# A pointwise convolution kernel: x's first chunk goes ahead of pw on SyncE's queue, one weight eviction is split between two engines, and weight copies are made once

## The chip, the cores and the metric

The kernel runs on one core of a Trainium2 chip. The metric is the device time of one execution in microseconds. The engines are TensorE (PE, with its weight loads shown as PEld), VectorE (DVE), ScalarE (ACT), GpSimd (POOL) and SyncE (SP), which here only issues DMAs.

## The reference

x is 1 x 384 x 384 x 384 in bf16 (147,456 pixels of 384 channels), dw is 1 x 1 x 384 and pw is 384 x 384. With k = 1 the depthwise step is one factor for each channel:

```
out = x * dw[0, 0]                             # one factor for each channel
return jnp.einsum('bhwc,cd->bhwd', out, pw)    # 384 x 384 matrix for each pixel
```

## The kernel before

The pixels are cut into 288 supertiles of 512. x is loaded in chunks of 1, 1, 1, 1, 2, 4, 5, 5 supertiles, then of 10, and of fewer at the end (`chunks`, from `_groups`), into three buffers `Xs`. VectorE transposes each supertile as 32-bit words in 32 x 32 blocks from X into `Ts` (lines 367 and 369), in two halves of three blocks; only the very first half is three instructions of one block each, with semaphores `s_t` and `s_tb`, so that PE may begin after the first block. PE does 48 matmuls for a supertile (line 225): 12 steps, each with four matmuls in four row groups of 32, which write the four banks of one half of PSUM (`PS[0]` or `PS[1]`, in turn). ScalarE evicts the four banks in one instruction into `Os` (line 429), and SyncE stores them.

The matmuls need the weights `w_r`: pw scaled by dw and spread over the row groups. They are made at the start. dw is loaded on ScalarE's queue, turned to a column by three small matmuls (line 255) and copied to `dw_f`. VectorE makes `sel_w`, a selection matrix scaled by dw, for each third k of the channels (line 400). PE multiplies it with pw (`pw_n`, which shares a tile named `raw` with `sel_w`) for k = 0, 1, 2 and r = 0, 1 (line 275): six pieces i = 2k + r, each of two banks, v = 0 and 1. The pieces go to PSUM and are evicted by `w_out` (line 385) into `w_r`; `w_eng` says which engine takes each piece (1 is ScalarE, 0 is VectorE; semaphores `s_wr`). Pieces 4 and 5 use the banks of pieces 0 and 1 and wait for their eviction. `times` makes PE do the two pieces of k = 2 twice over. The first supertile needs pieces 0 to 3 at its first step, piece 4 at its ninth step and piece 5 at its eleventh (`w_first`).

Before that, `idle_work` gives PE matmuls on constants (line 242): four rounds at the very start, two after the matmuls on dw. PE then waits for pw's first 128 rows (`s_pw`) and, ahead of k = 1, for the rest (`s_pw2`).

SyncE issues in this order: pw's first 128 rows (line 179), the rest of pw (line 180), x's chunk 0 (line 181, issued at line 133), x's chunks 1 to 5, then, after chunk 1 has landed, the rest of the loads and stores by a sorted list. Semaphores of a DMA count 16 at its landing.

On VectorE the order at the start is: `sel` (line 390), `dw_f` (397), `sel_w` (400), the weight pieces that are VectorE's, then the transposes of supertile 0 and of supertile 1. On ScalarE it is its weight pieces, then the evictions of the supertiles.

Of the kernel before, what the change touches and what calls it, by code (L numbers as in the profile page):

```python
# [26 lines left out]
def kernel(  # L27
# [12 lines left out]
    nc = tc.nc  # L40
# [38 lines left out]
    w_r = consts.tile([P, NB, 2, D], BF16, name="w_r")  # L79
# [31 lines left out]
    s_wr = [nc.alloc_semaphore(f"s_wr{e}") for e in range(2)]  # L111

    with tc.tile_critical(sync_engine=mybir.EngineType.Pool, no_gpsimd_drain=True):  # L113
        def x_of(t):
            g, i, off, first, L = chunks[t]
            if first + 2 == NS:
                return Xl[:], s_xl, 32
            n = sum(len(ls) > i for ls in groups[g % NR : g + 1 : NR])
            return Xs[g % NR][:, 4 * off : 4 * (off + L), :], s_x[g % NR][i], 16 * n

        def load_x(t, eng=nc.sync):
            g, i, off, first, L = chunks[t]
            dst, sem, _ = x_of(t)
            rows = xf[512 * first : 512 * (first + L), :]
            if first + 3 < NS:
                src = rows.rearrange("(p s) c -> p (s c)", p=P)
                dst = dst.rearrange("p s c -> p (s c)")
                if i == 0 and g >= NR:
                    je = g_end[g - NR]
                    eng.wait_ge(s_t[je % 2][1], je // 2 + 1)  # L130
            else:
                src = rows.rearrange("(a k q) c -> q a k c", k=4, q=4)
            eng.dma_start(dst, src).then_inc(sem, 16)  # L133
# [38 lines left out]
            eng = nc.scalar if first + 1 == NS and k == 2 else nc.sync  # L172
            eng.dma_start(dst, src).then_inc(s_o[g % NR], 16)

        w_eng = [1, 0, 1, 1, 1, 1]
        w_all = [(s_wr[e], w_eng.count(e)) for e in range(2)]

        nc.scalar.dma_start(dw_row[:], dw.rearrange("a e c -> a (e c)")).then_inc(s_dw, 16)
        nc.sync.dma_start(pw_n[:, 0], pw[0:P, :]).then_inc(s_pw, 16)  # L179
        nc.sync.dma_start(pw_n[:, 1:3], pw[P:C, :].rearrange("(k p) d -> p k d", p=P)).then_inc(s_pw2, 16)  # L180
        load_x(0)

        todo = []
        for t, (g, i, off, first, L) in enumerate(chunks):
# [12 lines left out]
        for o in sorted(range(NR), key=lambda o: (len(groups) - 1 - o) % NR):  # L197
            n = sum(n_parts[t] for t, c in enumerate(chunks) if c[0] % NR == o)
# [3 lines left out]

        w_done = [(s_wr[e], w_eng[: i + 1].count(e)) for i, e in enumerate(w_eng)]

        w_first = {(0, 0): [(0, 1), (1, 3)], (4, 0): [(1, 4)], (4, 1): [(1, 5)]}

        def w_ps(i):
            return PS[0 if i in (2, 3) else 1][:, 2 * (i % 2) : 2 * (i % 2) + 2, :D]  # L210
# [4 lines left out]
        def supertile(s, rv):  # L215
            for b, par in steps:
                for q in range(4):
                    if q == 0 and par == 0 and b in (0, 3):
                        nc.tensor.wait_ge(s_t[s][b // 3], rv)
                    if q == 0 and s == 0:  # L220
                        for e, v in w_first.get((b, par), []):
                            nc.tensor.wait_ge(s_wr[e], v)
                        if par == 0 and b in (1, 2):
                            nc.tensor.wait_ge(s_tb, b)
                    mm = nc.tensor.matmul(  # L225
                        PS[s][:, q, :D],
                        lhsT=Ts[s][32 * q : 32 * q + 32, b, par::2],
                        rhs=w_r[32 * q : 32 * q + 32, b, par, :],
                        start=(b, par) == steps[0],
                        stop=(b, par) == steps[-1],  # L230
                        tile_position=(32 * q, 0),
                    )
                    if (b, par) == steps[0] and q == 0:
                        mm._wait_ge(s_a[s], rv)
                    if (b, par) in ((2, 1), (5, 1)) and q == 3:
                        mm.then_inc(s_pe)


        def idle_work(n):
            for _ in range(n):  # L240
                for i in range(4):
                    nc.tensor.matmul(  # L242
                        PS[0][:, 2 * (i % 2) + i // 2, :D],
                        lhsT=ones[32 * i : 32 * i + 32, 0:P],
                        rhs=ones[32 * i : 32 * i + 32, :],
                        start=True,
                        stop=True,
                        tile_position=(32 * i, 0),
                    )
# [10 lines left out]
                stop=True,  # L260
            )
        mm.then_inc(s_df)
        idle_work(2)
        nc.tensor.wait_ge(s_pw, 16)
        times = {(2, 0): 2, (2, 1): 2}
        for k in range(3):
            if k == 1:
                nc.tensor.wait_ge(s_pw2, 16)
            nc.tensor.wait_ge(s_sw, k + 1)
            for r in range(2):  # L270
                if k == 2:
                    nc.tensor.wait_ge(*w_done[r])

                for v in [0, 1] * times.get((k, r), 1):
                    mm = nc.tensor.matmul(  # L275
                        PS[(k + 1) % 2][:, 2 * r + v, :D],
                        lhsT=sel_w[64 * v : 64 * v + 64, k, r, :, :].rearrange("p q w -> p (q w)"),
                        rhs=pw_n[64 * v : 64 * v + 64, k, :],
                        start=True,
                        stop=True,  # L280
                        tile_position=(64 * v, 0),
                    )
                mm.then_inc(s_w)
        with nc.tensor.Fori(0, NS // 2 - 1, 1) as it:
            rv = nc.tensor.to_reg(it + 1)
            for s in range(2):
                supertile(s, rv)
        supertile(0, NS // 2)

        Tk = Ts[1][:].rearrange("p b (i r) -> p (b i) r", r=2)  # L290
# [15 lines left out]
        for m in range(4):  # L306
# [14 lines left out]
            out=eye[:],  # L321
            in_=ones[:, 0:P],
# [20 lines left out]
        def transposes(t, j):  # L343
            g, i, off, first, L = chunks[t]
            jj = first + j
            s = jj % 2
            if jj + 1 == NS:
                nc.vector.wait_ge(s_xk, 32)
                Tw = Ts[s][:].bitcast(U32).rearrange("p b (m w) -> p (b m) w", w=32)
                for v in range(2):  # L350
                    blocks = slice(12 * v, 12 * v + 12)
                    ins = nc.vector.transpose(out=Tw[:, blocks], in_=Xk[:, blocks].bitcast(U32))  # L352
                    ins._wait_ge(s_pe, 2 * (jj - 2) + v + 1)
                    ins.then_inc(s_t[s][v])
                return
            X, sem, n = x_of(t)
            Xw = X.bitcast(U32).rearrange("p (k l) c -> p k l c", l=L)
            Tw = Ts[s][:].bitcast(U32).rearrange(
                "p b (k i) -> p b k i" if t < 2 else "p b (i k) -> p b k i", k=4
            )  # L360
            for h in range(2):
                if h == 0 and j == 0:
                    nc.vector.wait_ge(sem, n)
                if h == 0 and jj == 0:
                    for b in range(3):
                        x_b = Xw[:, :, 0, 32 * b : 32 * b + 32]
                        nc.vector.transpose(out=Tw[:, b], in_=x_b).then_inc(s_tb if b else s_t[0][0])  # L367
                    continue
                ins = nc.vector.transpose(  # L369
                    out=Tw[:, 3 * h : 3 * h + 3],  # L370
                    in_=Xw[:, :, j, 96 * h : 96 * h + 96].rearrange("p k (b w) -> p b k w", w=32),
                )
                if jj >= 2:
                    ins._wait_ge(s_pe, 2 * (jj - 2) + h + 1)
                ins.then_inc(s_t[s][h])
# [3 lines left out]

        order = [(t, j) for t in range(NT) for j in range(chunks[t][4])]  # L380

        def w_out(i):
            e, k, r = w_eng[i], i // 2, i % 2
            out, in_ = w_r[:, 2 * k : 2 * k + 2, r, :], w_ps(i)
            o = nc.vector.tensor_copy(out, in_) if e == 0 else nc.scalar.copy(out, in_)  # L385
            o._wait_ge(s_w, i + 1)
            o.then_inc(s_wr[e])
# [3 lines left out]
            out=sel[:],  # L391
            in_=eye[:].rearrange("p (v w r) -> p r w v", v=2, r=2),
# [6 lines left out]
        for k in range(3):  # L399
            nc.vector.tensor_scalar_mul(  # L400
                sel_w[:, k], sel[:].unsqueeze(2).to_broadcast([P, 2, 4, 32]), dw_f[:, k : k + 1]
            ).then_inc(s_sw)
        for i in range(6):
            w_out(i)
        transposes(*order[0])
        transposes(*order[1])

        for jj, (t, j) in enumerate(order):
            g, i, off, first, L = chunks[t]
# [28 lines left out]
            if jj + 2 < NS:  # L438
                transposes(*order[jj + 2])
# [30 lines left out]
```

## Time and profile before

| | |
|---|---|
| time before, median of 3 runs | 573.7 us (573.59 to 574.26) |
| profiled execution, span from the first to the last instruction | 572.6 us |
| profiled execution's own time | not given beside its span; the median of the runs is 1.1 us above the span |
| PE busy | 567.1 us, 99% of the span |
| DVE busy | 508.6 us, 89% |
| ACT busy | 418.3 us, 73% |
| DMA | 226.88 MB, mean 396 GB/s |
| first supertile's matmuls start | 6.45 us |
| second supertile's matmuls start | 9.02 us |

In the profile's rows times are microseconds unless marked ns. A row of the timeline has the start, the duration, the engine, the line of the kernel, the operation, the tiles written and read, the number of instructions merged into the row, and in brackets the engine's idle time before them with what ended it. A row of the chain of waits has start and duration. A row of the stretches has the stretch, its length, the busy time of PE, PEld, DVE, ACT and POOL with the number of instructions, the granted TensorE clock, the share of the DMA engines and the GB/s. A row of the DMA issues ends with the kilobytes of one and the median time from issue to landing. "SPq" is SyncE's queue of instructions. PE's matmuls are pipelined and their ends are modelled, so rows of PE overlap.

### The profile page before, as it was taken

What the parts mean: (1) busy time and instruction counts of PE and PEld (TensorE: products, weight loads), DVE (VectorE), ACT (ScalarE), POOL (GpSimd) and SP (SyncE); (2) the same over time, 40 slices, a digit from 0 to 9 for tenths busy, and PEclk for the clock granted to TensorE, in tenths of its full rate; (3) what the DMA queues carried; (4) which work ended last, traced back from release to release, by engine and by line L of the source; (5) the groups of instructions that cost most, each with busy time, mean ns of one, the idle gap of its engine ahead of it and who ended that gap; (6) DMA issues with size and microseconds to landing.
All of it is one profiled execution on the core that took longest, in us unless ns stands there. A gap on an engine that the chain in (4) does not pass through costs nothing.

```text
span 572.6 us, 29713 instructions
## 1 busy us (share of the span) xinstructions
PE 567.1 (99%) x13843; PEld 417.0 (73%) x13843; DVE 508.6 (89%) x588; ACT 418.3 (73%) x298; POOL 13.9 (2%) x41
## 2 busy tenths in 40 slices
PE   8999999999999999999999999999999999999997
PEld 4777777777777777777777777777777777777775
DVE  6999999999899899899899899899899899899895
ACT  6777777777777777777777777777777777777775
POOL 2042000000000000000000000000000000000000
PEclk9999999999999999999999999999999999999999
DMA  8999999999999999999999999999999999998777
GB/s 320 439 387 391 439 418 429 434 430 414 429 433 411 396 392 430 390 387 398 432 374 395 419 410 413 400 416 412 393 407 433 388 398 386 424 402 325 308 286 262
DMA packets 28084, 226.88 MB, mean 396 GB/s; under 512 B 1449, under 2 KB 7850, under 8 KB 24106
## 3 DMA queue, kind: packets, MB, share of 16 engines
q1 hardware_dynamic: 27140, 225.91, 97.5%
q10 hardware_dynamic: 934, 0.89, 0.4%
q14 instruction: 9, 0.07, 0.0%
q8 instruction: 1, 0.02, 0.0%
HBM read 113.54 MB, written 113.25 MB: 396 GB/s over the span
## 4 chain that ended last, share of the span: by engine, by line
PE 98%; DMA 1%; SPq 0%; issue 0%; DVE 0%; ACT 0%; POOLq 0%
PE ps L225 97%; DMA X<-in_x_dram 1%; PE ps L310 0%; PE ps L298 0%; DVE T L369 0%; ACT O L424 0%; SPq L133 0%; SPq L180 0%; SPq L179 0%; SPq L465 0%; POOLq L113 0%; POOLq L454 0%
## 5 line engine op out<-in xcount | busy, mean ns | idle before, releaser
L225 PE MATMUL ps<-w_r,T 32*128 32x384 bf16 x13776 | 560.0, 321 | 0.7 <-DVE T L369 0.4
L369 DVE STREAM_TRANSPOSE T<-X 128x384 uint32<-128x384 uint32 x571 | 500.6, 878 | 54.7 <-DMA X<-in_x_dram 1.1
L225 PEld LDWEIGHTS ps<-w_r,T 32*128 32x128 bf16 x13776 | 414.3, 93 | 146.6 <-issue 1.6
L429 ACT CAST O<-ps 128x1536 bf16<-128x1536 f32 x286 | 411.3, 1438 | 147.6 <-PE ps L225 147.6
L339 POOL COPY Xk<-Xl 32x256 bf16<-32x256 bf16 x16 | 6.3, 394 | 0.0
L338 POOL COPY Xk<-Xl 32x128 bf16<-32x128 bf16 x16 | 4.6, 287 | 25.5 <-DMA Xl<-in_x_dram 24.6
L385 ACT CAST w_r<-ps 128x768 bf16<-128x768 f32 x5 | 3.6, 820 | 0.8 <-PE ps L275 0.8
L333 POOL COPY raw<-w_r 32x768 bf16<-32x768 bf16 x4 | 3.3, 819 | 6.4 <-ACT w_r L385 6.2
L242 PE MATMUL ps<-const-bfloat16-1.0 32*128 32x384 bf16 x24 | 2.2, 515 | 1.1 <-PEq L454 1.1
L275 PE MATMUL ps<-raw 64*128 64x384 bf16 x16 | 2.8, 500 | 0.1
L275 PEld LDWEIGHTS ps<-raw 64*128 64x128 bf16 x16 | 0.8, 113 | 2.3 <-DMA raw<-in_pw_dram 1.2
L341 ACT ACT_TABLE_LOAD x1 | 1.3, 1283 | 1.5 <-PEq L454 1.5
L420 DVE CAST O<-ps 128x384 bf16<-128x384 f32 x2 | 1.0, 552 | 1.4 <-PE ps L225 1.4
L369 DVE STREAM_TRANSPOSE T<-Xl 128x384 uint32<-128x384 uint32 x2 | 1.8, 882 | 0.2
L242 PEld LDWEIGHTS ps<-const-bfloat16-1.0 32*128 32x128 bf16 x24 | 0.7, 117 | 1.4 <-issue 1.4
L390 DVE TENSOR_REDUCE sel<-eye 128x64 f32<-128x128 bf16 x1 | 0.3, 289 | 1.5 <-POOL eye L320 1.5
L352 DVE STREAM_TRANSPOSE T<-Xk 128x384 uint32<-128x384 uint32 x2 | 1.2, 578 | 0.5 <-PE ps L225 0.4
L310 PE MATMUL ps<-raw,T 128*128 128x384 bf16 x8 | 1.5, 328 | 0.0
L424 ACT CAST O<-ps 128x384 bf16<-128x384 f32 x2 | 1.0, 478 | 0.7 <-PE ps L310 0.7
L367 DVE STREAM_TRANSPOSE T<-X 128x128 uint32<-128x128 uint32 x3 | 0.7, 283 | 0.8 <-DMA X<-in_x_dram 0.8
L385 DVE CAST w_r<-ps 128x768 bf16<-128x768 f32 x1 | 1.0, 958 | 0.5 <-PE ps L275 0.5
L424 DVE CAST O<-ps 128x384 bf16<-128x384 f32 x2 | 1.1, 557 | 0.1
(14 smaller groups left out, 5.4 us busy)
## 6 DMA issues: line engine op xcount, KB each, us to landing
X<-in_x_dram SPq DMA_DIRECT2D x25, 3840.0 KB, 22.6
out_dram<-O SPq DMA_DIRECT2D x25, 3840.0 KB, 28.1
X<-in_x_dram SPq DMA_DIRECT2D x3, 1536.0 KB, 19.2
X<-in_x_dram SPq DMA_DIRECT2D x2, 1920.0 KB, 14.5
out_dram<-O SPq DMA_DIRECT2D x2, 1920.0 KB, 24.4
out_dram<-O SPq DMA_DIRECT2D x2, 1536.0 KB, 13.6
X<-in_x_dram SPq DMA_DIRECT2D x6, 384.0 KB, 6.4
out_dram<-O SPq DMA_DIRECT2D x3, 768.0 KB, 6.6
```

The costliest lines, as they stand in the source:

```text
L225: mm = nc.tensor.matmul(PS[s][:, q, :D], lhsT=Ts[s][32 * q : 32 * q + 32, b, par::2], rhs=w_r[32 * q : 32 * q + 32, b, par, :], start=(b, ...
L242: nc.tensor.matmul(PS[0][:, 2 * (i % 2) + i // 2, :D], lhsT=ones[32 * i : 32 * i + 32, 0:P], rhs=ones[32 * i : 32 * i + 32, :], start=True ...
L275: mm = nc.tensor.matmul(PS[(k + 1) % 2][:, 2 * r + v, :D], lhsT=sel_w[64 * v : 64 * v + 64, k, r, :, :].rearrange("p q w -> p (q w)"), rhs ...
L310: mm = nc.tensor.matmul(PS[1][:, m, :D], lhsT=Tk[:, P * (m + 2) : P * (m + 3), par], rhs=w_k[:, par, :], start=False, stop=par == 1,)
L333: nc.gpsimd.tensor_copy(w_k[quads[n]], w_r[quads[n], n]).then_inc(s_wk)
L338: nc.gpsimd.tensor_copy(Xk[quads[n], g:8:4, :], x_b).then_inc(s_xk)
L339: nc.gpsimd.tensor_copy(Xk[quads[n], 8 + g : 24 : 4, :], Xl[quads[g], :, 64 * n : 64 * n + 64]).then_inc(s_xk)
L341: nc.scalar.copy(warm[:, s : s + 1], nc.const_aps.tensor(0.0, [P, 1], F32)).then_inc(s_a[s])
L369: ins = nc.vector.transpose(out=Tw[:, 3 * h : 3 * h + 3], in_=Xw[:, :, j, 96 * h : 96 * h + 96].rearrange("p k (b w) -> p b k w", w=32),)
L385: o = nc.vector.tensor_copy(out, in_) if e == 0 else nc.scalar.copy(out, in_)
L424: o = (nc.scalar.copy if n % 2 else nc.vector.tensor_copy)(Ov[:, n, j, :], PS[s][:, n, :D])
L429: a = nc.scalar.copy(Ov[:, :, j, :], PS[s][:, :, :D])
```

## The change

x's chunk 0 is issued on SyncE's queue ahead of the two loads of pw instead of behind them. The fourth weight piece (i = 3) is evicted in two parts: its first bank by ScalarE, in ScalarE's order as before, its second by VectorE, between the first and the second block transpose of supertile 0; the waits of the first supertile count the two parts. The two pieces of k = 2 are multiplied once instead of twice, and the second `idle_work` has four rounds instead of two.

```diff
-        w_eng = [1, 0, 1, 1, 1, 1]
-        w_all = [(s_wr[e], w_eng.count(e)) for e in range(2)]
+        w_units = [(0, 0, 2, 1), (1, 0, 2, 0), (2, 0, 2, 1), (3, 0, 1, 1), (3, 1, 2, 0), (4, 0, 2, 1), (5, 0, 2, 1)]
+
+        def w_after(i):
+            n = [sum(u[3] == e and u[0] <= i for u in w_units) for e in range(2)]
+            return [(s_wr[e], n[e]) for e in range(2)]
+
+        w_all = w_after(5)
 
         nc.scalar.dma_start(dw_row[:], dw.rearrange("a e c -> a (e c)")).then_inc(s_dw, 16)
+        load_x(0)
         nc.sync.dma_start(pw_n[:, 0], pw[0:P, :]).then_inc(s_pw, 16)
         nc.sync.dma_start(pw_n[:, 1:3], pw[P:C, :].rearrange("(k p) d -> p k d", p=P)).then_inc(s_pw2, 16)
-        load_x(0)
...
-        w_done = [(s_wr[e], w_eng[: i + 1].count(e)) for i, e in enumerate(w_eng)]
-
-        w_first = {(0, 0): [(0, 1), (1, 3)], (4, 0): [(1, 4)], (4, 1): [(1, 5)]}
+        w_first = {(0, 0): w_after(3), (4, 0): w_after(4)[1:], (4, 1): w_after(5)[1:]}
...
-                        for e, v in w_first.get((b, par), []):
-                            nc.tensor.wait_ge(s_wr[e], v)
+                        for sem, v in w_first.get((b, par), []):
+                            nc.tensor.wait_ge(sem, v)
...
-        idle_work(2)
+        idle_work(4)
         nc.tensor.wait_ge(s_pw, 16)
-        times = {(2, 0): 2, (2, 1): 2}
         for k in range(3):
...
                 if k == 2:
-                    nc.tensor.wait_ge(*w_done[r])
-
-                for v in [0, 1] * times.get((k, r), 1):
+                    nc.tensor.wait_ge(*w_after(r)[1 - r])
+
+                for v in range(2):
...
                         nc.vector.transpose(out=Tw[:, b], in_=x_b).then_inc(s_tb if b else s_t[0][0])
+                        if b == 0:
+                            w_out(3, 1, 2, 0)
...
-        def w_out(i):
-            e, k, r = w_eng[i], i // 2, i % 2
-            out, in_ = w_r[:, 2 * k : 2 * k + 2, r, :], w_ps(i)
+        def w_out(i, v0, v1, e):
+            k, r = i // 2, i % 2
+            out, in_ = w_r[:, 2 * k + v0 : 2 * k + v1, r, :], w_ps(i)[:, v0:v1]
...
-        for i in range(6):
-            w_out(i)
+        for u in w_units:
+            if u[:2] != (3, 1):
+                w_out(*u)
```

## Prediction

> **What bounds the kernel now.** I read the page first, for the engine that fills the span. PE is busy 99% of it, and one group holds nearly all of that:
>
> ```profile
> PE 567.1 (99%) x13843; PEld 417.0 (73%) x13843; DVE 508.6 (89%) x588; ACT 418.3 (73%) x298; POOL 13.9 (2%) x41
> L225 PE MATMUL ps<-w_r,T 32*128 32x384 bf16 x13776 | 560.0, 321 | 0.7 <-DVE T L369 0.4
> ```
>
> Then the chain of waits that ended last, to see where PE stops being fed by itself:
>
> ```profile
> 1.87 0.46 SPq L133
> ...
> 2.38 5.89 DMA X<-in_x_dram
> ...
> 8.29 0.59 DVE T L369
> ...
> 9.02 557.88 PE ps L225 x13728
> 566.90 0.65 PE ps L298 x16
> ```
>
> From 9.02 us to 566.90 us PE never waits. Four matmuls with different row groups run together, so 13728 matmuls are 3432 groups of four, at 557.88 / 3432 = 0.1626 us each; a supertile of 512 rows is 12 groups, 1.95 us. The change touches nothing inside that stretch (the waits of the loop stay as many), nor the tail after it. So the whole question is one number: when the second supertile starts, now 9.02 us, and every tenth that this moves appears at the end of the kernel.
>
> The chain says that the second supertile waits for x's second chunk, issued at 2.38 and landed 5.89 us later, at 8.27. The timeline of the first 9 us shows what lies beside that (start, duration, engine, line; the bracket is the idle time before and its releaser):
>
> ```profile
> 0.96 0.39 SPq L179 DMA_DIRECT2D raw<-in_pw_dram  x1
> ...
> 1.12 1.47 PE L242 MATMUL ps<-const-bfloat16-1.0 32*128 32x384 bf16 x16 [1.12 <-PEq L454]
> ...
> 1.41 0.41 SPq L180 DMA_DIRECT2D raw<-in_pw_dram  x1
> ...
> 2.50 0.80 PE L242 MATMUL ps<-const-bfloat16-1.0 32*128 32x384 bf16 x5
> ...
> 3.37 2.83 PE L275 MATMUL ps<-raw 64*128 64x384 bf16 x16
> ...
> 3.91 3.61 ACT L385 CAST w_r<-ps 128x768 bf16<-128x768 f32 x5 [0.80 <-PE ps L275]
> 3.97 0.17 PEld L275 LDWEIGHTS ps<-raw 64*128 64x128 bf16 x4 [0.47 <-DMA raw<-in_pw_dram]
> 4.23 0.96 DVE L385 CAST w_r<-ps 128x768 bf16<-128x768 f32 x1 [0.48 <-PE ps L275]
> ...
> 6.04 0.70 DVE L367 STREAM_TRANSPOSE T<-X 128x128 uint32<-128x128 uint32 x3 [0.85 <-DMA X<-in_x_dram]
> ...
> 6.45 2.13 PE L225 MATMUL ps<-w_r,T 32*128 32x384 bf16 x48 [0.25 <-DVE T L367]
> 6.66 0.54 DVE L369 STREAM_TRANSPOSE T<-X 128x384 uint32<-128x384 uint32 x1
> ```
>
> The first supertile starts at 6.45, released by x's first chunk, and could hand over to the second at 6.45 + 1.95 = 8.40. It has 9.02 - 8.40 = 0.62 us of slack before x's second chunk stops being the bound: it may start as late as 7.07 at no cost.
>
> A second thing is in these rows: PE's pace.
>
> ```profile
> L242 PE MATMUL ps<-const-bfloat16-1.0 32*128 32x384 bf16 x24 | 2.2, 515 | 1.1 <-PEq L454 1.1
> 5.13 1.07 PE L275 MATMUL ps<-raw 64*128 64x384 bf16 x6
> ```
>
> The 16 matmuls of line 242 are 4 groups in 1.47 us, and with the 0.5 us of one matmul's own length (mean 515 ns) taken off, three steps take about 0.96, so 0.32 us a group, half the later speed. Line 225 at 6.45 does 11 steps in 2.13 - 0.32 = 1.81 us, 0.165 each. So between 1.12 and about 6 us PE runs at half speed, and from 6.45 at full speed. The column of the granted clock reads 1.00 throughout and does not show this; I go by the pace.
>
> **Part 1: x's first chunk ahead of pw.** What the queue gives, by size and by time to landing (each row is the one issue at 0.96, 1.41, 1.87, 2.38), and what the DMA engines moved per half microsecond:
>
> ```profile
> raw<-in_pw_dram SPq DMA_DIRECT2D x1, 96.0 KB, 2.0
> raw<-in_pw_dram SPq DMA_DIRECT2D x1, 192.0 KB, 2.5
> X<-in_x_dram SPq DMA_DIRECT2D x1, 384.0 KB, 4.1
> X<-in_x_dram SPq DMA_DIRECT2D x1, 384.0 KB, 5.9
> 2.00:2.50 0.50, 0.50 (x14) 0.21 (x10) 0.00 (x0) 0.50 (x1) 0.00 (x0) 1.00 0.66 174
> 2.50:3.00 0.50, 0.50 (x15) 0.10 (x7) 0.29 (x2) 0.49 (x3) 0.00 (x0) 1.00 0.81 186
> 3.00:3.50 0.50, 0.43 (x6) 0.16 (x4) 0.50 (x3) 0.11 (x2) 0.00 (x0) 1.00 1.37 313
> 3.50:4.00 0.50, 0.50 (x6) 0.03 (x4) 0.25 (x1) 0.09 (x1) 0.00 (x0) 1.00 0.71 169
> 4.00:4.50 0.50, 0.50 (x6) 0.14 (x4) 0.27 (x1) 0.50 (x1) 0.00 (x0) 1.00 0.85 344
> 4.50:5.00 0.50, 0.48 (x5) 0.16 (x4) 0.50 (x1) 0.50 (x2) 0.00 (x0) 1.00 1.50 320
> ...
> GB/s 320 439 387 391 439 418 429 434 430 414 429 433 411 396 392 430 390 387 398 432 374 395 419 410 413 400 416 412 393 407 433 388 398 386 424 402 325 308 286 262
> ```
>
> Three issues change places; their total is the same, so the second chunk of x, and all behind it, is still issued at 2.38 behind the same 672 KB. I take its landing as unmoved: 8.27. The last column of the half-microsecond rows (GB/s) summed from 2.0 gives 87, 180, 336, 421, 593, 753 thousand bytes at the ends of the six slices. Before, pw's first 98 thousand bytes were through by about 2.55 and landed at 2.96, and all 295 thousand of pw by 3.35 and landed at 3.9: landing comes 0.4 to 0.55 later. Now x's 393 thousand stand ahead: x plus the first part of pw, 491 thousand, is through by 4.2, so pw's first part lands at about 4.65 instead of 2.96; all 688 thousand are through by 4.8, so the rest lands at about 5.3 instead of 3.9. x itself lands near 4.3 instead of 6.0. Bounds for pw's first part: 3.9 (2.96 plus x's bytes at the 430 GB/s of the best slices of that row, 0.9 us); and 5.4, if x's tail holds it up as it held x: x's bytes were through at 4.8 and it landed at 6.0, 1.2 late. The value 4.65 is nearest to the two rows of pw itself.
>
> [...]
>
> **Part 2: the weights' path from pw's landing.** By the rows: the second part's weight load starts 0.05 us after its landing, so the first matmul of line 275 is at 4.70. ScalarE starts its first eviction 0.54 after (3.91 - 3.37): 5.24. Its five run at a pace of (3.61 - 0.82) / 4 = 0.70, so pieces 0, 2 and 3 start at 5.24, 5.94, 6.64. Piece 3 on ScalarE is now one bank:
>
> ```profile
> L385 ACT CAST w_r<-ps x5: 798/818/845, 3.9 to 6.7; 128x768 bf16<-128x768 f32 x5
> L420 DVE CAST O<-ps 128x384 bf16<-128x384 f32 x2 | 1.0, 552 | 1.4 <-PE ps L225 1.4
> L424 ACT CAST O<-ps 128x384 bf16<-128x384 f32 x2 | 1.0, 478 | 0.7 <-PE ps L310 0.7
> L367 DVE STREAM_TRANSPOSE T<-X x3: 269/269/311, 6.0 to 6.5; 128x128 uint32<-128x128 uint32 x3
> ```
>
> 0.48 us for one bank, done at 7.12 instead of 7.46. VectorE does piece 1 from 0.86 after the first matmul (4.23 - 3.37), 5.56 to 6.52; then the first transpose, about 0.27, then the other bank of piece 3, 0.55: done at about 7.3. Queued behind that bank on VectorE are transposes of blocks 1 and 2 and the second half; they are needed 0.33, 0.65 and 0.98 us into the first supertile and come in time. Pieces 4 and 5 end 0.34 earlier relative to pw and are needed later still. The first supertile starts at about 7.4: pw's landing plus 2.75. So the wait for x (6.04) is gone and the wait for the weights is late instead. The split saves only 0.16 (7.46 to 7.3), because the bank on VectorE ends last.
>
> At full speed the second supertile then starts at 7.4 + 1.95 = 9.35, 0.33 later than now.
>
> **Part 3: PE's idle work and the single copies.** Eight matmuls more of line 242 are two groups, 0.64 us, at 3.0 to 3.7, ahead of the wait for pw: they cost nothing, since pw lands after that. The repeated pairs of line 275 kept PE busy from 5.1 to 6.2 (the row of line 275 above); four fewer matmuls save no path time, since x held the start. What they gave was unbroken work: PE has no pause above 0.1 us from 1.12 to 6.20, and 4.9 us after its start or a little later it is at full speed. After the change PE stands still from 3.7 to 4.7 (1.0 us), then has single pairs, waiting for the rest of pw, for piece 0 to leave its banks (6.06) and for piece 1 (6.52), and nothing from about 6.9 to 7.4: a good half of the time from 3.7 to 7.4 is idle. If the count starts again at 4.70, full speed comes at about 9.6. The first supertile then does (9.6 - 7.4) / 0.32 = 6.9 groups slowly and 5.1 at 0.1626 (0.83 us): it ends at 10.43, 1.41 later than 9.02. Bounds of this term: 0.33 if the pauses don't matter; 2.2 if all 12 groups are slow (7.4 + 3.84 = 11.24). I take 1.4, since the only rows here that come to full speed come after unbroken work.
>
> [...]
>
> **Sum.** The profiled execution spans 572.6 us, 1.1 below the median of the runs, 573.7; that 1.1 lies around the span, and I keep it. 573.7 + 1.4 = 575.1. A measurement here can tell about 0.2%, 1.15 us, from no change, so this is only just slower.
>
> **Rivals.**
> No change: the clock doubles where it did, the pauses being too short to count. Then 573.7 + 0.33 = 574.0. For it: the two added groups of idle work shorten the pause. Against it: the pairs taken out. If the split of piece 3 does not do what it says, because the two engines get in each other's way at the same tile, it is 0.16 more, still no change.
> [...]
> Faster: the second chunk of x lands early and pw does too. It took 5.9 against 4.1 for an equal chunk just ahead, so 1.3 of it may be chance; if pw's first part lands at 3.9 the first supertile starts at 6.65 and the second at 8.60, 0.42 earlier: 573.3. It decides only if pw lands before 4.3 (first supertile before 7.07). Beyond 0.2% the second supertile would have to start at 7.87, so pw to land at 3.17; no row allows that. What remains for it is what I have not seen.
>
> **How the numbers follow.** Forecast 0.50 (0.44 of it above 0.2%), no change 0.30 (0.02 above), x's tail 0.10 (0.06 above), faster 0.10 (0.06 beyond 0.2%). That makes slower 0.52, same 0.42, faster 0.06. The forecast's own range is 574.4 (clock 3.4 us after pw) to 575.9 (all 12 groups slow). The whole range takes in the no-change case and the tail with the slow clock, 573.6 to 576.2.
>
> **What would show it.** In the profile after: x's first chunk landing near 4.3 and pw's first matmul (line 275) near 4.7; the first supertile released by a weight eviction and not by a transpose, near 7.4; its 48 matmuls over 3 us instead of 2.13; the second supertile near 10.4 with x's second chunk long landed at about 8.3. The prediction is wrong if the first supertile keeps 0.16 us a group, if pw lands before 4.3, or if the second supertile is still released by x.

## The result, and the profile after

The changed kernel takes 576.44 us (median of 6, 575.32 to 577.87) against 573.68 us (573.59 to 574.26): 1.0046 times as long, interval 1.0033 to 1.0059, or 2.8 us more. The profiled execution took 577.27 us and spans 575.2. It has a few lines more, so PE's supertiles stand at line 228 now, the weight pieces' matmuls at 277, their evictions at 389, the block transposes at 369.

The chain of waits of the kernel after (start, duration, what):

```profile
1.87 4.46 DMA raw<-in_pw_dram
6.33 0.05 issue
6.38 0.35 PE ps L277 x2
6.73 0.02 issue
6.76 1.19 ACT w_r L389 x2
7.94 0.14 issue
8.08 561.51 PE ps L228 x13776
```

x is gone from the chain. It is pw's second part, landing at 6.33 instead of 3.93, then two evictions, and from 8.08 to 569.59 PE without a pause: the second supertile no longer waits for x at all. The DMA issues at 0.96, 1.41, 1.87 and 2.34, one row each:

```profile
X<-in_x_dram SPq DMA_DIRECT2D x1, 384.0 KB, 3.0
raw<-in_pw_dram SPq DMA_DIRECT2D x1, 96.0 KB, 2.8
raw<-in_pw_dram SPq DMA_DIRECT2D x1, 192.0 KB, 4.5
X<-in_x_dram SPq DMA_DIRECT2D x1, 384.0 KB, 5.0
```

x's first chunk lands 2.1 us sooner (3.9), pw's parts 1.25 and 2.4 us later (4.2 and 6.33). And the timeline of the start:

```profile
2.50 1.44 PE L245 MATMUL ps<-const-bfloat16-1.0 32*128 32x384 bf16 x13
...
4.26 0.74 PE L277 MATMUL ps<-raw 64*128 64x384 bf16 x4 [0.32 <-DMA raw<-in_pw_dram]
...
6.38 0.82 PE L277 MATMUL ps<-raw 64*128 64x384 bf16 x8 [1.38 <-DMA raw<-in_pw_dram]
6.76 2.59 ACT L389 CAST w_r<-ps 128x768 bf16<-128x768 f32 x4 [1.16 <-PE ps L277]
6.92 0.56 DVE L389 CAST w_r<-ps 128x384 bf16<-128x384 f32 x1 [0.70 <-PE ps L277]
```

PE works from 4.26 to 5.00, stands still for 1.38 us, works to 7.20 and stands still again until 8.08. How its speed went is in the stretches (length, busy time of PE, ..., granted clock, DMA share, GB/s), cut where the trace's clock record changes (4.79, 8.20 and 11.61, so 3.41 us apart; the first row begins 3.41 ahead of the first change), and, last, the first supertile's matmuls alone:

```profile
1.38:4.79 3.41, 3.09 (x39) 1.19 (x31) 1.33 (x5) 1.57 (x3) 0.06 (x1) 1.00 0.71 195
4.79:8.20 3.41, 1.15 (x14) 0.46 (x16) 2.46 (x6) 2.24 (x4) 0.00 (x0) 1.00 1.00 329
8.20:11.61 3.41, 3.41 (x48) 2.15 (x44) 1.93 (x4) 1.14 (x2) 2.00 (x3) 0.50 1.05 438
...
8.08:11.70 3.62, 3.62 (x48) 2.33 (x52) 0.53 1.03 432
```

The stretch that is 3.09 / 3.41 = 0.91 busy is followed by full speed, the one that is 0.34 busy (1.15) by half speed, and the first supertile, begun at 8.08, runs nearly whole inside the half-speed stretch: 3.62 us instead of 1.95. This is the one place where the column of the granted clock shows it, 0.50: the record begins at the first change to full speed, and all before it reads 1.00. The second supertile starts at 11.70 instead of 9.02; that 2.7 is all of the difference of the two spans (2.6).

So two terms: late weights (the first supertile starts at 8.08 instead of 6.45, of which the wait for x's second chunk had hidden 0.62 in the kernel before) and a slow first supertile (1.67 us more). The experiments are there to tell them apart.

### The profile page after: what moved, and what is told of

The parts are those of the page before. It is cut to its first block, busy times and chain, and to the rows that moved or that the text cites. A ratio compares the mean times of both kernels' runs of the same rounds, so it can differ in the third digit from the quotient of the medians.

```text
span 575.2 us, 29722 instructions
## 1 busy us (share of the span) xinstructions
PE 567.9 (99%) x13847; PEld 418.1 (73%) x13847; DVE 507.3 (88%) x589; ACT 418.0 (73%) x298; POOL 13.9 (2%) x41
## 4 chain that ended last, share of the span: by engine, by line
PE 98%; DMA 1%; ACT 0%; SPq 0%; issue 0%; POOLq 0%
PE ps L228 98%; DMA raw<-in_pw_dram 1%; PE ps L312 0%; ACT w_r L389 0%; PE ps L300 0%; ACT O L429 0%; SPq L185 0%; SPq L133 0%; PE ps L277 0%; SPq L470 0%; POOLq L113 0%; POOLq L459 0%
## 5 line engine op out<-in xcount | busy, mean ns | idle before, releaser
L389 ACT CAST w_r<-ps 128x768 bf16<-128x768 f32 (+1 forms) x5 | 3.4, 747 | 2.8 <-PE ps L277 2.8
L389 DVE CAST w_r<-ps 128x768 bf16<-128x768 f32 (+1 forms) x2 | 1.5, 758 | 2.0 <-PE ps L277 2.0
L277 PE MATMUL ps<-raw 64*128 64x384 bf16 x12 | 1.6, 374 | 1.7 <-DMA raw<-in_pw_dram 1.7
```

The costliest lines, as they stand in the source:

```text
L277: mm = nc.tensor.matmul(PS[(k + 1) % 2][:, 2 * r + v, :D], lhsT=sel_w[64 * v : 64 * v + 64, k, r, :, :].rearrange("p q w -> p (q w)"), rhs ...
```

## The experiments

**The parts one at a time.** The order alone, in the kernel before:

```diff
+        load_x(0)
         nc.sync.dma_start(pw_n[:, 0], ...)
         nc.sync.dma_start(pw_n[:, 1:3], ...)
-        load_x(0)
```

> The kernel before with one edit: x's chunk 0 is issued ahead of pw. Piece 3 whole on ScalarE, the repeated pairs of the last third and two rounds of idle work stay. Theory (late pw plus pauses of PE that put its clock at half speed): pw's second part lands at 6.0 to 6.4 as in the changed kernel, the first supertile starts at 8.1 to 8.5, and some or all of its groups take 0.32 us, so the second starts near 11.7: 575.5 to 577. Rival A (the single copies cost the time, the order does not): pauses are short because the repeats are there, full pace at the first supertile, second supertile at 10.0 to 10.4: 574.7 to 575.1. Rival B (the split eviction costs the time): 573.7.

Measured: 575.69 us (574.59 to 577.04, 10 runs), 1.0028, interval 1.0016 to 1.0040. In its profile pw landed at 4.5 and 5.0, so the second part came soon after the first there. The first supertile started at 7.48 and the second at 10.31. PE was at half speed up to 9.30, which cost 0.9 us (2.84 instead of 1.95). Rival A's repeats did not keep the speed. One row of its waits shows a cost that no one had named:

```profile
PEld ps L255 <- DMA dw_row<-in_dw_dram: 1.4, 1, 1.4
```

dw's 768 bytes, on ScalarE's queue, landed 1 us later with x first, and PE paused for it: its weight load of dw starts at 3.29, against 2.29 in the kernel before. In the kernel after the same wait is 0.4. All but the order, in the changed kernel:

```diff
-        load_x(0)
         nc.sync.dma_start(pw_n[:, 0], ...)
         nc.sync.dma_start(pw_n[:, 1:3], ...)
+        load_x(0)
```

> The changed kernel with x's chunk 0 back behind pw; split eviction, single copies and four rounds of idle work stay. Theory: pw lands at 3.0 and 3.9 again, x at 6.0, the first supertile starts at 6.4; PE stands still only from about 5.7 to 6.4, so the pace is full at the first supertile and x's second chunk releases the second supertile near 9.0: 573.7, within 0.4. Rival A (the single copies cost the time): the clock is late here too, 575 or more. Rival B (the split costs it): 574.5 or more with a full pace.

Measured: 575.09 us (10 runs), 1.0014, interval 1.0002 to 1.0027, and the median means little: five executions lie at 574.07 to 574.35, five at 575.83 to 575.97. The profile is of one of the longer five; none of the shorter five has one. pw landed at 2.9 and 3.8, the first supertile started at 6.69, and all 48 matmuls were slow:

```profile
3.72:7.13 3.41, 2.94 (x24) 1.01 (x24) 2.43 (x7) 2.72 (x5) 0.00 (x0) 1.00 1.00 345
7.13:10.54 3.41, 3.41 (x52) 1.89 (x47) 2.08 (x4) 0.58 (x1) 2.51 (x4) 1.00 1.06 433
...
6.69:10.48 3.79, 3.79 (x48) 2.14 (x52) 1.00 1.05 422
```

With the loads as before, 2.94 / 3.41 = 0.86 busy did not bring full speed; it came at 10.54, a full stretch later. The shorter five are 1.7 us faster. That the stretches fell otherwise there fits the numbers, but is not shown without a profile of them. My expectation (573.7 within 0.4) held for two executions and was missed by 0.3 at most in three more; in the other half it failed. The order alone (1.0028) and all the rest alone (1.0014) together come near the whole (1.0046). Next, the repeats alone taken out of the kernel before:

```diff
-        times = {(2, 0): 2, (2, 1): 2}
+        times = {}
```

> The kernel before with one edit: the pairs of the last third are multiplied once instead of twice. Loads, evictions and idle work stay, so nothing on the path to the first supertile moves. Theory, as the first four runs leave it: TensorE's speed is set anew every 3.41 us by how busy PE was; shares of 0.91 and more brought full speed, 0.86 and less did not. Without the repeats PE pauses from about 5.8 to 6.4, so a 3.41 us stretch that holds the pause is 0.80 to 0.88 busy: some executions stay as before (573.7 to 574.2) and some begin the first supertile at half speed (575.4 to 575.9), as in the run with all but the order. Rival (repeats are nothing but copies, the spread of that run came from the split): all executions at 573.7 to 574.2.

Measured: 575.17 us (573.78 to 577.03, 10 runs), 1.0024, interval 1.0009 to 1.0039: four executions at 573.8 to 574.1, six at 575.2 to 577.0. The rival falls, since the interval lies above 1: taking work off PE that nobody waited for made the kernel slower in more than half of its executions. The kernel before was not steady beside it either: 6 of its 25 executions are above 575.0. The slowest are slower than I allowed for (575.9), and no profile shows those. In the profiled one, which took 573.85, PE was busy for 2.95 us of the stretch from 0.73 to 4.14 (0.86), and the first supertile took 1.95. The split alone:

```diff
-        idle_work(4)          # the changed kernel, with order and repeats put back
+        idle_work(2)
...
-                for v in range(2):
+                for v in [0, 1] * {(2, 0): 2, (2, 1): 2}.get((k, r), 1):
```

> The changed kernel with the order of loads, the repeated pairs and the two rounds of idle work as before: what is left is the split of the fourth weight piece. Theory: x's chunk still releases the first supertile, the weights are ready earlier and nobody waits for them; PE is as busy as before: 573.6 to 574.2 in all executions. Rival (the split itself costs): 575 or more, or two groups of times.

Measured: 574.32 us (573.69 to 576.33, 10 runs), 1.0004, interval 0.9988 to 1.0019. Five of ten executions are as expected; three are above 574.8, as are 6 of the 25 of the kernel before beside it. The split costs nothing that can be told.

**The clock alone.** The kernel before without its idle work:

```diff
-        idle_work(4)
-
         nc.tensor.wait_ge(s_dw, 16)
...
-        idle_work(2)
```

> The kernel before without any idle work, six rounds taken out; loads, weights and repeats as before. The path to the first supertile is the same: pw at 3.0 and 3.9, x at 5.7 to 6.0. Theory: PE's busy time begins at 3.4 instead of 1.1, so the first 3.41 us stretch that is 0.9 busy ends between 6.5 and 9.9; the first supertile starts at 6.4 to 6.5, in most executions at half speed: 573.8 to 575.5, spread evenly, median near 574.7. This is the clock alone. Rival (PE's speed changes at its own time, whatever PE did): 573.7 to 574.2.

Measured: 574.46 us (574.02 to 575.82, 10 runs), 1.0010, interval 1.0000 to 1.0020. The median is a little under what I expected and hardly clear of the kernel before beside it; two executions lie above the 575.5 that I allowed. Its profile is of one of the longer ones (575.25): first supertile at 6.14, even sooner than before, second at 9.73.

```profile
2.67:6.08 3.41, 2.83 (x16) 0.74 (x16) 2.47 (x8) 2.72 (x7) 0.00 (x0) 1.00 0.98 305
6.08:9.50 3.42, 3.42 (x46) 1.84 (x48) 2.45 (x5) 1.32 (x2) 1.83 (x3) 1.00 1.03 408
```

0.83 busy, no full speed until 9.50. Nothing on the path came later; in this execution the time went into PE's pace.

**Filling PE's pauses in the changed kernel.** The first try put a fixed block of six rounds in the wait for pw:

```diff
             if k == 1:
+                idle_work(6)
                 nc.tensor.wait_ge(s_pw2, 16)
...
+                for v in [0, 1] * {(2, 0): 2, (2, 1): 3}.get((k, r), 1):
```

> The changed kernel with PE kept at work in its pauses: six rounds of idle work between the first third's pairs and the wait for the rest of pw, and the pairs of the last third made two and three times over. Nothing else moves; the loads are as in the changed kernel. Theory: pw's second part still lands near 6.3 and the first supertile starts near 8.1 to 8.3, but at 0.16 us a group, so the second starts near 10.1 instead of 11.7: 574.5 to 575, some 1.6 faster than the changed kernel. Rival (the late pw alone is the loss, the clock follows its own time): 576.4, no change.

Measured: 576.95 us (575.46 to 578.44, 8 runs), 1.0043, interval 1.0029 to 1.0058: a miss. The profile is of the slowest of the eight executions (578.44). The first supertile did run at full speed there (1.95 us), but it started at 9.33: pw's second part landed at 5.0 and PE was in its idle rounds until 7.5. The filling stood in the way. The second try used shorter pieces:

```diff
-        idle_work(4)
+        idle_work(6)
...
             if k == 1:
+                idle_work(1)
...
+                for v in [0, 1] * {(2, 0): 2, (2, 1): 2}.get((k, r), 1):
```

> The changed kernel with PE's pauses filled by short pieces that stand in nobody's way: six rounds of idle work instead of four ahead of pw, one round between the first third and the wait for the rest of pw, the repeats of the last third back. Loads and split as in the changed kernel. Theory: pw lands at 4.2 to 4.5 and 5.0 to 6.3, the first supertile starts at 7.2 to 8.2 and runs at full speed, so only the late pw is left: second supertile at 9.2 to 10.1, 574.4 to 575.3, 1.3 to 2 faster than the changed kernel. Rival (the loss is the late weights and their chain, and the clock comes too late anyway): 576 to 577.

Measured: 576.52 us (575.88 to 576.97, 4 runs), 1.0042, interval 1.0026 to 1.0059: over the 574.4 to 575.3 that I expected, and no better than the changed kernel. In the profile the start is as expected: first supertile at 7.78 at full speed, second at 9.73. But the span is 574.9, and its tail, the time behind PE's last matmul, is 5.2 us, against 3.5 in the kernel after. The DMA queue of instructions in the last 6 us and the last store, of this kernel, and then the last store of the kernel after:

```profile
q8 instruction: 1, 0.02, 1.0%
...
out_dram<-O ACTq DMA_DIRECT2D x1, 96.0 KB, 3.6
```

```profile
out_dram<-O ACTq DMA_DIRECT2D x1, 96.0 KB, 1.9
```

A 16 KB fetch of instructions falls into the tail, and the last store lands 1.7 us later beside it; the kernel after has no such fetch there. The first filled kernel shows such a fetch too and a tail of 5.2, but there it is SyncE's last stores that land late (192 KB take 3.4 us instead of 1.9) and the very last store took 2.4, not the 3.6 that the next expectation says of both. Both programs have over 30 instructions more than the changed kernel, a weight load counted with each matmul. So I made the program shorter, each idle round one matmul of 128 rows:

```diff
-            for _ in range(n):
-                for i in range(4):
-                    nc.tensor.matmul(PS[0][:, ...], lhsT=ones[32 * i : 32 * i + 32, 0:P], ...)
+            for i in range(n):
+                nc.tensor.matmul(PS[0][:, i % 4, :D], lhsT=ones[:, 0:P], rhs=ones, start=True, stop=True)
```

> The changed kernel with PE's pauses filled as in the last filled kernel, but each round of idle work is one matmul of 128 rows instead of four of 32, so the program has fewer instructions than the changed kernel. In the two filled kernels before, the last store landed 3.6 us after its issue instead of 1.9, beside a 16 KB fetch of instructions in the tail; with the shorter program that fetch should not fall there and the tail should be 3.5 us again. Theory: first supertile at 7.2 to 8.2 and at full speed in nearly all executions, only the late pw is left: second supertile at 9.2 to 10.1, 574.4 to 575.4, 1 to 2 faster than the changed kernel beside it. Rival (the late weights are the whole loss): as the changed kernel, 576 to 577.

Measured: 576.27 us (575.02 to 577.68, 11 runs), 1.0036, interval 1.0027 to 1.0045: another miss, over the 574.4 to 575.4 expected, but the tail was 3.5 us and the fetch gone from it. Its profile is of one of the slowest executions (577.67). There dw was late again (PE waited 1.4 us for it), pw's second part landed at 7.1, and the stretch from 4.30 to 7.71 was 2.94 / 3.41 = 0.86 busy: no full speed before 11.13. One execution in which the loads were this late says little on the others, so this left the question open. The version that says most keeps the second try and shortens only the very first four rounds:

```diff
-        idle_work(4)
+        for i in range(4):
+            nc.tensor.matmul(PS[0][:, i, :D], lhsT=ones[:, 0:P], rhs=ones, start=True, stop=True)
```

> The filled kernel of the second group (six rounds ahead of pw, one between the thirds, repeats back) with only the very first four rounds as single matmuls of 128 rows, so that it has 8 instructions more than the changed kernel instead of 32, and the 16 KB fetch of instructions should not fall into the tail. Theory: that kernel's 575.9 to 577.0 less the 1.7 of its tail, so 574.2 to 575.4 with a tail of 3.5 us; the first supertile at 7.3 to 8.2, at full speed in most executions. If dw lands late behind x's packets, as in the short filled kernel (3.3 instead of 2.25), PE pauses all the same and it is 576 or more. Rival (the pauses don't matter): 576.4 as the changed kernel.

Measured: 575.22 us (574.64 to 576.74, 11 runs), 1.0027, interval 1.0018 to 1.0036. Nine of the 11 executions lie at 574.6 to 575.5, two at 576.6 and 576.7. Of 13 executions of the changed kernel two are under 575.6. The profile has late weights and full speed, and a tail of 3.5 us, the fetch falling behind the last instruction:

```profile
2.01:5.42 3.41, 3.41 (x37) 1.23 (x35) 1.04 (x4) 1.35 (x4) 0.00 (x0) 1.00 0.84 231
...
7.35:9.30 1.95, 1.95 (x48) 1.44 (x52) 1.00 1.05 425
```

So with PE filled the change costs 575.22 - 573.77 = 1.45 us against the kernel before beside it, and the rest of the 2.8, some 1.3, is PE's speed. The two intervals (1.0018 to 1.0036, 1.0033 to 1.0059) overlap at their ends, and two of the 11 executions are as long as the changed kernel's.

**pw on a queue of its own.** The changed kernel with pw on ScalarE's queue:

```diff
-        nc.sync.dma_start(pw_n[:, 0], ...)
-        nc.sync.dma_start(pw_n[:, 1:3], ...)
+        nc.scalar.dma_start(pw_n[:, 0], ...)
+        nc.scalar.dma_start(pw_n[:, 1:3], ...)
```

> The changed kernel with the two loads of pw issued on ScalarE's queue, behind dw's, while x's chunk 0 is first on SyncE's. The theory says that the loss begins with pw queued behind x's bytes: with a queue of its own pw shares the DMA engines with x instead of following it. If the first part lands by 3.8 and the second by 4.8, the first supertile starts near 7.0, PE's pauses are short, and the second starts by 9.0: 573.2 to 574.2. If the bytes of x on the same 16 DMA engines delay pw as much from another queue, pw lands at 4.2 and 6.3 again and it is 575.5 to 577.

Measured: 580.49 us (579.93 to 580.79, 4 runs), 1.0103, interval 1.0085 to 1.0122: worse than both cases that I had written down.

```profile
raw<-in_pw_dram ACTq DMA_DIRECT2D x1, 192.0 KB, 7.7
raw<-in_pw_dram ACTq DMA_DIRECT2D x1, 96.0 KB, 4.9
...
11.55 4.69 PE L228 MATMUL ps<-w_r,T 32*128 32x384 bf16 x68 [0.41 <-ACT w_r L389]
```

pw landed at 6.4 and 9.6: not behind one chunk of x but beside several, since SyncE goes on issuing. From 0.9 to 4 us ScalarE's queue moved 22 packets and SyncE's 238, 0.02 and 0.68 MB, so a packet had some 0.9 KB on the one and 2.9 KB on the other. The first supertile started at 11.55 and was slow as well: its eviction began 3.93 us later, against 2.18 in the kernel before. Here another queue was no way past x's bytes.

**The best that the runs point to.** The order of loads as before, split and repeats kept, and PE filled with single matmuls:

```diff
-        idle_work(2)          # the split-only kernel, idle rounds as one matmul each
+        idle_work(3)
...
             if k == 1:
+                idle_work(1)
```

> The best version that the runs point to: loads in the order of before, the split kept (weights are ready sooner), repeats kept, idle work as single matmuls of 128 rows, three rounds instead of two ahead of pw and one between the thirds, so that PE has no long pause from 1.1 us to the first supertile. Theory: first supertile at 6.1 to 6.5 at full speed, second at 8.3 to 8.9: 573.5 to 574.0, at or just under the kernel before, with fewer late executions. Rival (the spread is that of the loads): 573.7 to 575.5, as before.

Measured: 574.15 us (573.97 to 576.15, 12 runs), 1.0006, interval 0.9998 to 1.0015. Eleven of 12 executions lie within 0.6 us, but none under 573.97: in the profile the fillings delay the weights (first supertile at 6.81). It does not beat the kernel before.

**Are the profiles typical?** The changed kernel again, twice, and the kernel before once more:

> The changed kernel unchanged, for the comparison on the same chip in the same rounds. Theory and rivals alike: 575.3 to 577.9, median near 576.4; its first supertile runs at half speed wholly or in part in most executions.

> A third profile of the changed kernel, to see which of its terms repeat. Theory: pw's second part lands at 5.0 to 6.4, the first supertile starts at 7.4 to 8.1, and its 48 matmuls take 2.8 to 3.8 us instead of 1.95 where the stretches of 3.41 us before it were under 0.86 busy. Rival: full speed and still 576.

> A second profile of the kernel before. The first one shows the second supertile at 9.02, held by x's second chunk at 8.27; but most executions of it span 571.7 to 572.3, less than the 572.6 of that profile. Theory: typically x's second chunk lands by 7.5 and the second supertile follows the first without a wait at 8.35 to 8.5, so the loss of the changed kernel is to be counted from there: span 571.7 to 572.2. Rival: 9.0 again, 572.6.

Measured: the changed kernel 576.72 us (575.02 to 577.55, 6 runs; 1.0046, interval 1.0033 to 1.0059) and 576.66. The two new profiles agree with each other: pw's second part at 5.90 and 5.86, the first supertile at 7.81 and 7.77, its 48 matmuls in 3.20 and 3.22 us, full speed from 10.39. The third profile's stretches and its first supertile:

```profile
3.57:6.98 3.41, 2.27 (x17) 0.57 (x12) 1.57 (x4) 1.33 (x2) 0.00 (x0) 1.00 0.88 274
6.98:10.39 3.41, 3.00 (x40) 1.53 (x40) 2.60 (x7) 2.05 (x4) 1.15 (x2) 1.00 1.06 432
...
7.77:10.99 3.22, 3.22 (x48) 1.90 (x52) 1.00 1.06 440
```

0.67 busy, no full speed; then 0.88 busy, full speed. The kernel before took 573.81 us and spans 572.1. Its chain, and the busy stretch ahead of full speed:

```profile
1.41 3.04 DMA raw<-in_pw_dram
...
6.68 559.83 PE ps L225 x13776
```

```profile
2.65:6.06 3.41, 3.04 (x22) 0.89 (x16) 2.63 (x9) 2.27 (x6) 0.00 (x0) 1.00 0.99 314
```

Here x's second chunk is not in the chain: the first supertile starts at 6.68 and the second follows at 8.63 without a wait. Nor is x's first chunk: the first supertile waits for the weights already in the kernel before, and the change makes that wait longer. The first profile of the kernel before, with x's second chunk at 8.27, was the odd one. The 23 executions beside the first four experiments span 572.0 in the median, against 572.6.

Side by side the profiles tell the two terms apart (times in us):

| kernel | pw's second part lands | first supertile starts | its 48 matmuls | second supertile starts | span |
|---|---|---|---|---|---|
| before, second profile | 4.45 | 6.68 | 1.95 | 8.63 | 572.1 |
| order alone | 5.02 | 7.48 | 2.84 | 10.31 | 573.8 |
| all but the order | 3.82 | 6.69 | 3.79 | 10.48 | 574.0 |
| changed, first | 6.33 | 8.08 | 3.62 | 11.70 | 575.2 |
| changed, second | 5.90 | 7.81 | 3.20 | 11.01 | 574.5 |
| changed, third | 5.86 | 7.77 | 3.22 | 10.99 | 574.4 |
| filled, second try | 5.87 | 7.78 | 1.95 | 9.73 | 574.9, with 1.7 more of tail |

Counted from the first row, the later start of the second supertile is in each row the difference of the spans, to 0.1 us, with the tail taken off in the last. The last three rows are the closest pair: in the second filled kernel pw happened to land as in the second and third profile of the changed kernel, and the first supertile started at the same time, so that the whole difference up to the second supertile, 1.27 us, is PE's pace. PE's matmuls of the supertiles, busy in all, in the third profile and in the filled kernel:

```profile
L228 PE MATMUL ps<-w_r,T 32*128 32x384 bf16 x13776 | 561.1, 321 | 0.4 <-ACT w_r L389 0.4
L228 PE MATMUL ps<-w_r,T 32*128 32x384 bf16 x13776 | 559.8, 321 | 0.6 <-ACT w_r L390 0.6
```

What is left, 7.78 against 6.68, is the late weights: 1.1 us in these executions, and 1.4 in the first profile, where the pace took 1.67.

## Why the prediction was right and wrong

The sign was right, and so was one mechanism: after PE's pauses the first supertile ran slowly (3.62, 3.20 and 3.22 us instead of 1.95). The other, the wait for x that turns into a wait for the weights, describes the first profile of the kernel before; in the second the weights were waited for already, and the change made them later. The size was half of what it is (1.4 forecast, 2.8 measured), and 576.44 lies above the range that I gave (576.2).

The step that failed most is the sum's reference. I took the span of one profile, 572.6, and the median of other executions, 573.7, for one and the same execution, "1.1 lies around the span". The runs show the time and the span of each execution: what lies around the span is 2.0 us in the median, before (23 executions) and after (6) alike, and the kernel before usually spans 572.0. The profile that I built on was slow by 0.6. My forecast for the span, 572.6 + 1.4 = 574.0, with 2.0 around it would have been 576.0; the changed kernel's spans have a median of 574.45. So 0.9 of the 1.3 us that were missing is this step; the other 0.45 is weights that came later and a pace that was slow for longer than forecast.

With it goes the slack. "It may start as late as 7.07 at no cost" held for that one execution. In the second profile the first supertile hands over to the second with none, so that late weights cost from the first tenth on.

pw's landing: first part forecast 4.65, measured 4.2 to 4.4; second part forecast 5.3, measured 6.33, 5.90, 5.86. I put the upper bound on the first part and let the path to the first supertile start there, 2.75 us after its landing; but that landing set nothing. My own sign of being wrong, pw before 4.3, came true in two of the three profiles (4.21 and 4.20) while the time went up: the chain goes through the second part, and the first supertile starts 1.75 to 1.9 us after that. Hence the first supertile at 8.08, 7.81 and 7.77 and not at 7.4. In the first profile the three loads landed in the order of issue, at 3.9, 4.2 and 6.33. The upper bound of 5.4 for pw's first part, x's tail holding pw up, was an estimate that no run shows: that part landed at 4.2 to 4.4, and x had landed whole 2.4 us before pw's second part. Why that part took 4.0 to 4.5 us from issue to landing, and 3.2 in the order-only kernel, is open. x's own chunk, with nothing ahead of it, took 3.0 us instead of 4.1.

The slow pace: forecast 1.08 us, measured 1.67, 1.25 and 1.27. I restarted the count when PE's work restarted, at 4.70, and so had full speed at 9.6; it came at 11.6 and 10.4. That restart was an estimate of mine, and the first profile does not bear it out: there PE had been at full speed from 4.79 and lost it at 8.20. The lower end of my own range, 574.4, takes full speed 3.4 us after pw, and no run shows that term: in the three profiles of the changed kernel the first supertile came to full speed 7.4, 6.0 and 6.1 us after pw's first matmul. In the profiles the speed after such a stretch of 3.41 us went with PE's busy share in it: 0.88 or more was followed by full speed each time, 0.83 or less never, and 0.86 once and not twice. The stretches began at another point in each profile (2.55 and 2.65 in the two of the kernel before, 1.38, 3.56 and 3.57 in the three of the changed one).

The split: forecast to save 0.16, and the last weight was VectorE's bank in the forecast. In the profile ScalarE's bank ends last (7.94, VectorE's 7.48), since VectorE had been free since 6.22. The two evictions of ScalarE in the chain take 1.19 us, against 1.51 in the second profile of the kernel before, so here the split saved some 0.3. Taken alone it moves nothing.

The single copies: "four fewer matmuls save no path time" was right, and what was lost with them is what I said, busy time. Alone they cost 1.0024 (1.0009 to 1.0039).

Of the chances given, the 0.10 for x's tail, and with it the range's upper end, rested on pw landing at 5.4 behind x, a term that no run shows: it was pw's own second part that was late. No change and faster fell.

What stays open: the shares of the two terms are known to some tenths only (1.25 to 1.7 us for the pace, 1.1 to 1.45 for the weights, and 0.7 in the profile of the last filled kernel, whose first supertile starts at 7.35), since no kernel holds pw's landing fixed and the closest pair is one execution by chance; why pw's second part is so late; and why executions without the repeats reach 577.0, which no profile shows.

## What to carry to other kernels

Before adding a difference to a median, see whether the profile and the median are the same execution: compare the span of the profile with the spans of the timed runs, and count slack only if two profiles show it. A load that the first consumers share with a longer chain of work (here the weights: PE, two engines' evictions, PE again; behind x, the first supertile started at 7.77 to 8.08 instead of 6.68) goes ahead of the one whose consumer follows at once. Work on an engine that nobody waits for can still be worth its time, as the repeats were here (1.0024 without them): take out matmuls near the start only after counting the busy share of PE in the stretch before the first real work.

## What the runs showed of the hardware

In the first profile of the changed kernel TensorE's granted clock changes at 4.79, 8.20 and 11.61 us, at intervals of 3.41. Counted back from the change to full speed in steps of 3.41, the stretches begin 2.55 us after the span's start in the first profile of the kernel before, 1.38 in the first of the changed one and 0.15 in its second. The record of the clock has one long time at full speed, of 566.6 us in the first profile of the kernel before and 563.2 in the first of the changed one, which is 166 and 165 times 3.413; in the former the first supertile ran at full pace (0.165 us a group), in the latter it took 3.62 us. One stretch more at half speed is worth half of 3.41, 1.7 us by this estimate, and 1.7 us is also the distance of the two groups of times in the kernel with all but the order (574.2 and 575.9), of which only the longer was profiled. The recorded clock reads 1.00 ahead of its first change although a group of four matmuls takes 0.32 us there instead of 0.163.

With x first on SyncE's queue, PE's weight load waited 1.4 us for dw's 768 bytes on ScalarE's in three of eight profiles (the order-only kernel and two of the filled ones), against 0.4 to 0.6 in the other five (three of the changed kernel, pw on ScalarE's queue, and the last filled one).

The longer programs had a longer end: in the two kernels with over 30 more instructions a 16 KB fetch of instructions fell among the last stores, and the tail was 5.2 us instead of 3.5; in one of them the last store took 3.6 us instead of 1.9. In the two later filled kernels, which have fewer instructions than these, the fetch was absent from the tail, or fell 1.7 us behind the last instruction, and the store took 1.9 again. That it is the fetch that delays the stores was not tried otherwise.
